# Retention and gated convolution on one core: a SyncE wait between a visit's y groups, whole columns in unit 0, and a new order from a corrected planner

## The chip, the cores and the metric

One core of one Trainium2 chip. The metric is the device time of one execution in microseconds; of several runs the median counts.

## The reference

Two stages, cut to what matters. First a retention layer with 4 batches, 8 heads, 768 tokens and 64 dimensions; then a gated MLP on its output, with 512 channels:

```python
for t in range(S):
    state = gamma * state + einsum('bhd,bhe->bhde', k[:, :, t], v[:, :, t])
    y[:, :, t] = scale * einsum('bhd,bhde->bhe', q[:, :, t], state)
x = y.transpose(0, 2, 1, 3).reshape(B, S, H * D)
gate = sigmoid(causal_conv(x, conv_w))        # five taps, each channel alone
out = (gate * (x @ w_val)) @ w_out
```

All inputs and the output are float32.

## The kernel before

The 768 tokens are cut into six chunks of 128, and with four batches that makes 24 pairs of batch and chunk, g = 0 to 23, taken chunk by chunk. All four batches of one chunk are a unit of 512 tokens for the MLP, so there are six units.

*Retention.* A pair of chunk 0 (g = 0 to 3) has a short form: `first_scores` (32 small products), a mask on VectorE, `first_y` (32 products), an evacuation into x on VectorE (`evac`), and `first_state`. Every later pair is a **visit**: `visit` does the 32 products of the masked scores with v, y's first group (`y_scores`, line 480 in the trace), then 16 products that complete this pair's state and 16 for the next pair's (line 464); then `rest_of_visit` adds y's second group, 32 products of the state with q (`y_state`, line 480 as well, since both call `y_mm`), and the next pair's 32 scores (line 407). In chunk 5 a visit has only the next pair's 16 state products, and the last visit has none. Both groups add into the same PSUM columns, from different rows of the array, so the second may begin only when the first is complete. The step `turn` sees to that: ScalarE copies two columns of y into a small tile that nobody reads, and TensorE waits for it.

*The MLP.* x is split into a high and a low part of TensorE's fast float32 format: ScalarE casts (`round_x`), GpSimd subtracts (`rest_x`). Four val tiles for each unit (`val_tile`) have 12 matmuls of 512 columns each: high by high, low weight by high, high weight by low. Unit 0 is in HALVED: its tiles are made as 24 matmuls of 256 columns (`val_half`, line 706), the first 12 of which need batches 0 and 1 alone. The convolution has one tap on ScalarE and four on VectorE (line 679), then comes a sigmoid on ScalarE, and VectorE multiplies it into the val tile's bank (line 715). The gated tile is split again. Units 0 and 5 have four output tiles (line 820); units 1 to 4 have seven products of half size (line 777), which need sums of blocks of w_out (`t_sums_at`) and buffers named top, from which the result is also sent. Two PSUM banks named mm serve val tiles, products and output tiles in turn.

*Loads.* SyncE issues all loads but two small ones. `LOADS` is the list of the first ones: ("q", g) is a pair's q and transposed k (0.5 MB), ("v", g) and ("k", g) 0.25 MB each, ("w", n) a weight block (0.5 MB; 0 to 3 are w_val's, 4 to 7 w_out's), "t" the table of masks and decays. A visit's step is followed by the two loads of the pair four ahead, and before the first of them stands a tiny DMA named passed (line 374), which makes SyncE wait until the visit has been evacuated.

*The order* of every engine is written out when the kernel is built. `WORK` is a string with one letter for each block of work: s, y, z for the first scores, y and state, p for the position product, w a weight load, h the head of the first visit, v a visit, V a val tile, T the sums of w_out, O an output tile or product. It gives each step a due time; `plan` then lists all steps as a simulation with the constants at the top of the file places them, and puts fillers (products into unused columns) into TensorE's gaps in the first stage. `fetch` and `run_pe` are its model of TensorE's instruction supply.

Of the kernel before, what the change touches and what calls it, by code (L numbers as in the profile page):

```python
# [7 lines left out]
F32 = mybir.dt.float32  # L8
# [8 lines left out]
P = 128  # L17
# [16 lines left out]
LO, HI = slice(0, HALF), slice(HALF, P)  # L34
# [1 line left out]

PAIR = 0.0145
MM = 0.2325
INTO, OUT_OF = 0.3, 0.134
COLD, WARM_AT = 1.85, 5.0  # L40
FIRST_PAGE, PAGE = 71, 127.6
FETCH, AHEAD, BEHIND, WORST = 3.3, 0.5, 1.5, 6.5
FIRST_BYTE, PER_MB = 2.95, 2.52
LATE_MB, LATE = 0.75, 1.85
TABLES = (4.6, 4.6)
SENT, SLACK = (2.8, 0.4), 1.5
HALVED = (0,)

TIMES = {
    "DVE": (0.69, 0.60),  # L50
# [8 lines left out]
FILLED_VALS = 48  # L59
CONV_LEAD, CHUNK = 7.0, 3.4  # L60
LOADS = (
    ("q", 0), ("t", 0), ("q", 1), ("v", 0), ("q", 2), ("w", 3), ("w", 0), ("v", 1),
    ("v", 2), ("v", 3), ("q", 3), ("k", 0), ("w", 1), ("w", 2), ("k", 2), ("k", 1),
    ("k", 3),
)

WORK = (
    "sspysyysyzzwzVwwhvVVzVwvOOOTvOvVvvVVvvVOVVvV"
    "VOvOOvvOOOOVVVvOOvOOOOvVvVOVvOOOVVvOOvOOOvVO"
    "OOVOVVOOOOO"  # L70
)

SEEN = {"DVE": 0.035, "ACT": 0.035, "POOL": 0.08, "PE": 0.08}
# [31 lines left out]
def plan(steps, filler, last, into):  # L105
# [46 lines left out]
    left = [0] * len(steps)  # L152
# [8 lines left out]
    while ends:  # L161
        t = ends.pop()
# [17 lines left out]
        if not s.waits:  # L180
            offer(s)
    order, landed, moved = [], 0.0, 0.0
    left, crossed, kind, sent = float(FIRST_PAGE), -9.0, "big", []

    def fetch(now):

        nonlocal left, crossed
        queued = max((x for t, x in sent if t <= crossed + AHEAD), default=0.0)
        crossed = now = max(now, min(max(crossed + FETCH, queued + BEHIND), crossed + WORST))
        left += PAGE  # L190
        return now

    def run_pe(s, now):
        nonlocal left, kind
        slow = COLD if now < WARM_AT else 1.0
        if s.small:
            if kind == "big":
                now += INTO
            kind = "small"
            todo, each = s.small, PAIR * s.wide * slow  # L200
        else:
            if kind == "small":
                now += OUT_OF
            kind = "big"
            todo, each = s.big, s.gap / max(1, s.big) * slow
        while todo > left:
            now += left * each
            todo -= left
            left = 0.0
            now = fetch(now)  # L210
        left -= todo
        now += todo * each
        return now, now + (0.21 if s.small else 0.17) * slow

# [2 lines left out]
    def quiet(ring):  # L217

        ends = [[s.end for s in users[k]] for k, w in rings.get(ring, ()) if w.end is not None]
        return max((1e9 if e is None else e for x in ends for e in x), default=0.0)  # L220

    def offered(e):
        return free[e] if e != "PE" or held is None else [s for s in free[e] if s is held]
# [18 lines left out]
    while any(free.values()):  # L242
        start, _, e = min(
            (round(max(clock[e], min(max(s.ready, s.own if s.engine == e else 0.0) for s in offered(e))), 6), e, e)
            for e in free
            if offered(e)
        )
        s = min(
            (s for s in offered(e) if max(s.ready, s.own if s.engine == e else 0.0) <= start + 1e-6),
            key=lambda s: (round(s.rank, 6), s.index),  # L250
        )
        if e == "PE":
            held = s.hold
            shut = shut or s.shut
            filling = filling and s is not last and s.hold is None
            ring = min(into[shut:], key=quiet)
            since = max(clock["PE"], quiet(ring))
            for i in range(int((start - since) * FILLED / FILL) if filling else 0):
                f = Step(0, "PE", FILL, [], [], filler, (ring,))
                f.start = since + i * FILL  # L260
                f.end = f.free = f.start + FILL
                order.append(f)
                left = max(0.0, left - (2 if ring == into[0] else 4))
        free[s.engine].remove(s)
        if s.other:
            free[s.other[0]].remove(s)
            if s.engine != e:
                s.engine, (s.cost, s.gap), s.fn = s.other
        s.start = start
        order.append(s)  # L270
        if e == "PE":
            clock[e], end = run_pe(s, start)
        elif e == "DMA":
            clock[e] = start + 0.45
            if moved <= LATE_MB < moved + s.mb:
                landed += LATE
            moved += s.mb
            landed = end = max(landed, start + FIRST_BYTE) + s.mb * PER_MB
            sent.append((start, landed))
            end += SLACK * (start > 30.0)  # L280
        else:
            if s.two:
                start = s.start = max(start, clock["POOL"])
                clock["POOL"] = max(clock["POOL"], start + s.gap)
            clock[e], end = start + s.gap, start + s.cost
            if s.mb:
                landed = max(landed, start + FIRST_BYTE - 0.6) + s.mb * PER_MB
                sent.append((start, landed))
        done(s, end)
        if s.turn:  # L290

            t, e = s.turn, s.turn.engine
            free[e].remove(t)
            t.start = max(clock[e], start + 0.49 + 32 * PAIR)
            clock[e] = t.start + t.gap
            order.append(t)
            done(t, t.start + t.cost)
# [5 lines left out]
def tile_retention_gated_mlp(  # L303
# [9 lines left out]
    nc = tc.nc  # L313
# [7 lines left out]
    const = ctx.enter_context(tc.tile_pool(name="const", bufs=1))  # L321
# [7 lines left out]
    ps_a = ctx.enter_context(tc.tile_pool(name="ps_a", bufs=2, space=PSUM))  # L329
    ps_m = ctx.enter_context(tc.tile_pool(name="ps_m", bufs=2, space=PSUM))  # L330

    turned = const.tile([P, 2, 1], F32, name="turned")
    small_sb = const.tile([P, small.shape[1]], F32, name="small_sb")
    vd_sb = small_sb[:, 0:48].rearrange("p (c x) -> p c x", x=8)
    ra_sb = small_sb[:, 48:72].rearrange("p (c x) -> p c x", x=4)
# [13 lines left out]
    sy = ps_y.tile([P, 2, 512], F32, name="sy")  # L349
# [10 lines left out]
    def at(due, engine, cost, reads, writes, fn, *args):  # L360
        steps.append(Step(due, engine, cost, list(reads), list(writes), fn, args))
        return steps[-1]
# [164 lines left out]
    def turn(g):  # L527


        nc.scalar.copy(turned[HI], sy[HI, :, 256:257])  # L530

    def rest_of_visit(g):
        y_state(g)
# [385 lines left out]
    def attention(g, t):  # L919

        b, c = chunks[g]
        qk, vk = ("att", g % LB, "qk"), ("att", g % LB, "vk")
        u, y = us_of.pop(g), Slot("y", 1)
        n = 32
        if g + 1 < NG:
            decay_at(t - 0.01, g + 1)
            taken[g + 1] = [Slot("snap", 4), Slot("snap", 4)]
            at(t - 0.005, "ACT", TIMES["snap"], ["z"], taken[g + 1][0:1], snap, g + 1, 0)
            n += 16
        if c < NCH - 1:  # L930
            n += 16
        step = at(t, "PE", 1.0, [u, vk] + ([("att", (g + 1) % LB, "vk")] if g + 1 < NG else []), [y, "z"], visit, g)
        step.small = n
        step.turn = at(t + 0.5, "ACT", (0.25, 0.2), [y], ["turn"], turn, g)
        reads, writes = [qk, "turn"] + taken[g], [y]
        if g + 1 < NG:
            scored[g + 1] = Slot("sc", 1)
            reads.append(("att", (g + 1) % LB, "qk"))
            writes.append(scored[g + 1])
        step.hold = at(t + 1.0, "PE", 1.0, reads, writes, rest_of_visit, g)  # L940
        step.hold.small = 64 if g + 1 < NG else 32
        if g + 1 < NG:
            scored_at(t + 1.01, g + 1)
        if b == 0:
            xbufs[c] = Slot("x", XB)
            last = [xbufs[c - 1]] + [("x", c - 1, i) for i in range(B)]
            at(t + 0.5, "ACT", (0.25, 0.15), last, [xbufs[c]] + [("x", c, i) for i in range(B)], new_x, c)
        at(t + 1.9, "DVE", TIMES["DVE"], [y, ("dec", c % 2), xbufs[c]], [("x", c, b)], evac, g)
        if c + 1 < NCH:
            at(t + 2.4, "ACT", (0.4, 0.3), ["base", "small"], [("dec", (c + 1) % 2)], table, c + 1, b)  # L950
        split(c, b, t + 1.95)
        whole[c] = t + 2.0
# [73 lines left out]
    def val_tile(n, m, t):  # L1026
        bank = Slot("mm", 2)
        gate_of = gates[n, m]
        halved = n in HALVED
        for z in range(3 * NPAIR * (1 + halved)):  # L1030
# [127 lines left out]
    for p, (kind, n) in enumerate(LOADS):  # L1158
        t = 0.1 * p
        if kind == "t":  # L1160
            at(t, "DMA", 0.4, [], ["small"], get, small_sb, small, nc.sync).mb = 0.2
        elif kind in "qrvk":
            load_part_at(t, n, *{"q": (0, 2), "r": (2, 4), "v": (2, 3), "k": (3, 4)}[kind])
        else:
            load_w_at(t, n)
# [12 lines left out]
    t, whole = 6.0, {}  # L1178
    now = dict.fromkeys("psyzvVOT", 0)
    now["h"] = now["v"] = B  # L1180
    now["w"] = len(early)
    for what in WORK:
# [7 lines left out]
        elif what == "s":  # L1190
            t = max(t, 6.0 + CHUNK * i)
# [138 lines left out]
```

## Time and profile before

| | |
|---|---|
| median of 3 runs | 207.59 us (205.69 to 209.82) |
| profiled execution | 206.92 us |
| its span, first to last instruction | 205.1 us |
| TensorE busy | 196.1 us, 96% |
| VectorE, ScalarE, GpSimd busy | 64%, 55%, 68% |
| DMA | 36.28 MB, mean 177 GB/s |

The span is what the trace shows; 1.8 us of the execution lie around it. Matmuls overlap, and their ends are modelled, so how fast a group of them runs is read from the starts of its members, or from the chain of waits, where each piece ends at the next one's start.

### The profile page before, as it was taken

The numbers are of one execution on the slowest core, as the hardware profiler recorded it, in microseconds if no ns is written. First come the engines' busy times: TensorE is split into PE (matmuls) and PEld (weight loads), VectorE is DVE, ScalarE is ACT, GpSimd is POOL, SyncE is SP. The second block draws the span as 40 slices with busy tenths as digits, with TensorE's granted clock in tenths as the row PEclk, the third lists the DMA queues.
The fourth block names the chain that finished last, engine by engine and source line by source line (L and its number), as shares of the span: only waits on it lengthen the run. The fifth ranks groups of instructions, "written<-read, shape, count | busy, mean of one in ns | idle before, by whom it ended". The sixth has DMA issues, their size and how long they took to land.

```text
span 205.1 us, 8324 instructions
## 1 busy us (share of the span) xinstructions
PE 196.1 (96%) x3688; PEld 167.4 (82%) x3688; DVE 131.2 (64%) x200; ACT 113.6 (55%) x245; POOL 140.1 (68%) x120
## 2 busy tenths in 40 slices
PE   8888989999999999999999899999999999999994
PEld 2576878878888879888999689988888889888883
DVE  1375987930489968992559795559992448994100
ACT  4198699754697558862555824236682237612221
POOL 0049949999997784999999738248999199222500
PEclk9999999999999999999999999999999999999999
DMA  6999994385595756344069520779001013112022
GB/s 199 367 410 411 414 415 168 107 291 227 151 328 176 270 211 220 135 141 190 3 225 316 189 96 6 258 187 328 5 13 44 0 54 105 51 63 91 0 105 104
DMA packets 14648, 36.28 MB, mean 177 GB/s; under 512 B 1554, under 2 KB 6034, under 8 KB 14612
## 3 DMA queue, kind: packets, MB, share of 16 engines
q1 hardware_dynamic: 8816, 29.43, 40.1%
q10 hardware_dynamic: 5796, 6.32, 8.7%
q8 instruction: 29, 0.48, 0.9%
q14 instruction: 7, 0.06, 0.1%
HBM read 29.46 MB, written 6.29 MB: 174 GB/s over the span
## 4 chain that ended last, share of the span: by engine, by line
PE 74%; DMA 17%; DVE 4%; ACT 1%; issue 1%; SPq 1%; ACTq 0%; DVEq 0%
PE mm L694 28%; PE mm L777 18%; PE mm L820 11%; PE sy L480 11%; DMA qk<-in_att_dram 6%; DMA wst<-in_w_dram 5%; PE sy L407 4%; DMA vk<-in_att_dram 4%; PE z_ps L464 4%; DMA out_dram<-top 2%; DVE acc L679 2%; SPq L383 1%; DVE u L429 1%; DVE x L622 1%; DVE x L560 0%
## 5 line engine op out<-in xcount | busy, mean ns | idle before, releaser
L679 DVE SCALAR_TENSOR_TENSOR acc<-x,cw_sb,acc 128x512 f32<-128x512 f32 x96 | 67.8, 751 | 4.3 <-ACT acc L677 3.7
L575 POOL TENSOR_TENSOR xl<-x,xh 128x512 fp32r<-128x512 f32 x24 | 31.0, 1291 | 22.9 <-ACT xh L570 22.9
L762 POOL TENSOR_TENSOR gvl<-gate,gvh 128x512 fp32r<-128x512 f32 x24 | 30.8, 1293 | 9.2 <-ACT gvh L758 9.2
L396 POOL TENSOR_TENSOR vk<-vk,small_sb 128x512 f32<-128x512 f32 x24 | 25.1, 1047 | 1.9 <-PE z_ps L464 1.3
L694 PE MATMUL mm<-xl,wvh 128*128 128x512 f32 x80 | 25.8, 395 | 0.0
L560 DVE TENSOR_TENSOR x<-sy,dec 128x512 f32<-128x512 f32 x20 | 13.7, 687 | 18.7 <-PE sy L407 17.7
L694 PE MATMUL mm<-xh,wvh 128*128 128x512 f32 x80 | 25.5, 403 | 0.0
L715 DVE TENSOR_TENSOR gate<-mm,gate 128x512 f32<-128x512 f32 x24 | 16.4, 688 | 13.7 <-PE mm L694 11.3
L694 PE MATMUL mm<-xh,wvl 128*128 128x512 f32 x80 | 24.2, 399 | 0.0
L745 POOL TENSOR_TENSOR gate<-gate 128x512 f32<-128x512 f32 x16 | 20.6, 1292 | 3.9 <-DVE gate L715 3.7
L758 ACT CAST gvh<-gate 128x512 fp32r<-128x512 f32 x24 | 14.7, 625 | 13.2 <-DVE gate L715 10.0
L570 ACT CAST xh<-x 128x512 fp32r<-128x512 f32 x24 | 14.9, 621 | 8.2 <-DVE x L560 7.3
L687 ACT ACTIVATE gate<-acc 128x512 f32<-128x512 f32 x24 | 14.3, 599 | 8.7 <-DVE acc L679 4.5
L726 POOL TENSOR_TENSOR gvl<-gate,gvh 128x512 fp32r<-128x512 f32 x8 | 10.3, 1290 | 12.6 <-ACT gvh L722 12.6
L694 PEld LDWEIGHTS mm<-xh,wvl 128*128 128x128 f32 x80 | 14.8, 188 | 3.3
L694 PEld LDWEIGHTS mm<-xl,wvh 128*128 128x128 f32 x80 | 14.9, 188 | 3.0
L429 DVE TENSOR_TENSOR u<-sy,small_sb 128x512 f32<-128x512 f32 x20 | 13.7, 685 | 5.6 <-PE sy L407 5.6
L677 ACT ACTIVATE acc<-x,cw_sb 128x512 f32<-128x512 f32 x24 | 16.4, 691 | 1.4 <-DVE x L560 1.1
L694 PEld LDWEIGHTS mm<-xh,wvh 128*128 128x128 f32 x80 | 14.3, 188 | 3.2
L530 ACT COPY turned<-sy 64x2 f32<-64x2 f32 x20 | 3.1, 156 | 23.5 <-PE sy L480 17.7
L475 ACT COPY snap<-z_ps 128x256 f32<-128x256 f32 x40 | 14.2, 376 | 3.2 <-PE z_ps L464 1.6
L464 PE MATMUL z_ps<-vk 64*64 64x64 f32 x704 | 14.8, 219 | 0.4 <-issue 0.4
(83 smaller groups left out, 410.6 us busy)
## 6 DMA issues: line engine op xcount, KB each, us to landing
qk<-in_att_dram SPq DMA_DIRECT2D x24, 512.0 KB, 5.7
vk<-in_att_dram SPq DMA_DIRECT2D x20, 512.0 KB, 5.0
wst<-in_w_dram SPq DMA_DIRECT2D x8, 512.0 KB, 8.4
out_dram<-o_sb ACTq DMA_DIRECT2D x15, 256.0 KB, 2.7
vk<-in_att_dram SPq DMA_DIRECT2D x8, 256.0 KB
out_dram<-top ACTq DMA_DIRECT2D x8, 256.0 KB, 4.2
passed<-x SPq DMA_DIRECT2D x16, 0.0 KB
out_dram<-gate ACTq DMA_DIRECT2D x2, 128.0 KB, 1.7
```

What stands on the lines that cost most here:

```text
L396: nc.gpsimd.tensor_tensor(v, v, vd_sb[:, c, :].unsqueeze(2).broadcast_to([P, 8, HALF]), op=ALU.mult)
L464: nc.tensor.matmul(z_ps[cols, x, b, j], lhsT=k[rows, x, j, s, :], rhs=v[rows, x, j, s, :], start=g == 0 and s == 0 and j == 0, stop=True, ...
L480: nc.tensor.matmul(sy[cols, h, off:off + HALF], lhsT=lhsT, rhs=rhs, start=start, stop=True, skip_group_check=True,)
L575: nc.gpsimd.tensor_tensor(xl[n][:, :, b], xs[n][:, :, b, HALO:], xh[n][:, :, b].bitcast(F32), op=ALU.subtract)
L677: nc.scalar.mul(acc, x[:, :, 0:P], cw_sb[:, m, 0:1])
L679: nc.vector.scalar_tensor_tensor(acc, x[:, :, k:k + P], cw_sb[:, m, k:k + 1], acc, op0=ALU.mult, op1=ALU.add,)
L694: nc.tensor.matmul(vps[n, m], lhsT=w[:, m, ct * P:(ct + 1) * P], rhs=xx[n][:, ct].rearrange("p b t -> p (b t)"), start=(i == 0), stop=(i = ...
L715: nc.vector.tensor_tensor(gv, vps.pop((n, m)), gv, op=ALU.mult)
L745: engine.tensor_tensor(block(n, k), block(n, a), block(n, b), op=getattr(ALU, op))
L762: engine.tensor_tensor(low, block(n, k), operands[n, k, 0].bitcast(F32), op=ALU.subtract)
L777: nc.tensor.matmul(banks[bank][:, tt * 256:(tt + 1) * 256], lhsT=g[:, ct, tt * P:(tt + 1) * P], rhs=weight(w, part % 2)[:, ct], start=(k i ...
L820: nc.tensor.matmul(ops[n, b, cs.start][:, 0:cs.stop - cs.start], lhsT=gg[:, b * P:(b + 1) * P], rhs=w[:, ct, cs], start=(i == 0), stop=(i ...
```

## The change

- `turn` no longer copies. An empty SyncE instruction reads the same two columns, as far as dependences go; TensorE's second group waits for SyncE's semaphore. The planner counts the step on the DMA queue, at 0.1 us in place of ScalarE's 0.25.
- HALVED is empty: unit 0's val tiles use 512 columns like the others.
- The planner's model of the instruction supply is another (fetches are asked for at a page's end and become usable later), its constants for loads and for the small table are changed.
- LOADS and WORK are other orders of the same steps.

```diff
-INTO, OUT_OF = 0.3, 0.134
+INTO, OUT_OF = 0.25, 0.134
-FETCH, AHEAD, BEHIND, WORST = 3.3, 0.5, 1.5, 6.5
-FIRST_BYTE, PER_MB = 2.95, 2.52
-LATE_MB, LATE = 0.75, 1.85
+LEAD, AHEAD, BEHIND, WORST, USABLE, DEPTH = 1.0, 0.0, -0.95, 4.5, 2.35, 23
+FIRST_BYTE, PER_MB = 2.85, 2.65
+LATE_MB, LATE = 1.0, 1.7
-SENT, SLACK = (2.8, 0.4), 1.5
-HALVED = (0,)
+SENT, SLACK = (3.4, 0.4), 0.7
+HALVED = ()
 LOADS = (
-    ("q", 0), ("t", 0), ("q", 1), ("v", 0), ("q", 2), ("w", 3), ("w", 0), ("v", 1),
-    ("v", 2), ("v", 3), ("q", 3), ("k", 0), ("w", 1), ("w", 2), ("k", 2), ("k", 1),
-    ("k", 3),
+    ("q", 0), ("t", 0), ("q", 1), ("w", 0), ("q", 2), ("v", 1), ("v", 0), ("v", 2),
+    ("v", 3), ("q", 3), ("w", 1), ("k", 1), ("k", 0), ("w", 2), ("k", 3), ("w", 3),
+    ("k", 2),
 )
 WORK = (
-    "sspysyysyzzwzVwwhvVVzVwvOOOTvOvVvvVVvvVOVVvV"
-    "VOvOOvvOOOOVVVvOOvOOOOvVvVOVvOOOVVvOOvOOOvVO"
-    "OOVOVVOOOOO"
+    "spssyysyyzwVzwVVwwzzhVvOOvvOvOVvTVvVvVvOVVOv"
+    "vVvOOOVvOVOVOvOOOVvOOOvvVOVVVOOOOOvOOOOvOvO"
+    "vVOVOVVOOOO"
 )
...
     def fetch(now):
-        nonlocal left, crossed
-        queued = max((x for t, x in sent if t <= crossed + AHEAD), default=0.0)
-        crossed = now = max(now, min(max(crossed + FETCH, queued + BEHIND), crossed + WORST))
-        left += PAGE
+        nonlocal left, need, usable, later
+        if left <= 1e-9:
+            asked = max(now, usable)
+            queued = max((x for t, x in sent if t <= asked + AHEAD), default=0.0)
+            later = min(max(asked + LEAD, queued + BEHIND), asked + WORST) + USABLE
+            left = PAGE
+        else:
+            now = max(now, usable)
+            usable, need = later, PAGE
         return now
...
     def turn(g):
-        nc.scalar.copy(turned[HI], sy[HI, :, 256:257])
+        nc.sync.keepalive_nop([nc.sync.lower_ap(sy[HI, :, 256:257])])
...
-        step.turn = at(t + 0.5, "ACT", (0.25, 0.2), [y], ["turn"], turn, g)
+        step.turn = at(t + 0.5, "DMA", (0.1, 0.0), [y], ["turn"], turn, g)
...
-            at(t, "DMA", 0.4, [], ["small"], get, small_sb, small, nc.sync).mb = 0.2
+            at(t, "DMA", 0.4, [], ["small"], get, small_sb, small, nc.sync).mb = 0.07
```

Written out by blocks (V1.2 is unit 1's third val tile, O2.0 unit 2's first product, v8 the visit of g = 8), the new order begins s p s s y y s y y z w V0.0 z w V0.1 V0.2 w w z z h V0.3 v4 O0.0 O0.1 v5 v6 O0.2 v7 O0.3 V1.0, where the old one has s s p y s y y s y z z w z V0.0 w w h v4 V0.1 V0.2 z V0.3 w v5 O0.0 O0.1 O0.2 T v6 O0.3 v7 V1.0. Around the end of unit 1 the old one has O1.4 O1.5 O1.6 O2.0 V3.0, the new one O1.5 V3.0 O1.6 V3.1 O2.0. Neighbouring visits are v5 v6, v12 v13 and v18 v19 in the new order; O3.6 O4.0 are neighbours in both.

## Rows read from the trace of the kernel before

**Rows 1.** The page: busy us by engine, and the chain that ended last.
```profile
PE 196.1 (96%) x3688; PEld 167.4 (82%) x3688; DVE 131.2 (64%) x200; ACT 113.6 (55%) x245; POOL 140.1 (68%) x120
...
PE 74%; DMA 17%; DVE 4%; ACT 1%; issue 1%; SPq 1%; ACTq 0%; DVEq 0%
```

**Rows 2.** Busy time by stage: stretch, length, engines' busy us, clock, DMA share, GB/s.
```profile
5.00:20.00 15.00, 12.65 (x283) 9.60 (x283) 7.85 (x13) 9.80 (x22) 6.41 (x6) 1.00 1.02 394
20.00:42.10 22.10, 20.87 (x530) 19.12 (x530) 18.98 (x29) 18.48 (x38) 19.02 (x17) 1.00 0.71 275
42.10:202.10 160.00, 158.34 (x2878) 137.31 (x2870) 103.50 (x158) 82.77 (x180) 114.44 (x95) 1.00 0.42 144
```

**Rows 3.** The start in order of time: start us, us, engine, line, tiles, [idle <-releaser].
```profile
10.85 0.90 PE L497 MATMUL z_ps<-u,vk 64*64 64x128 f32 x32
...
15.94 1.23 PE L420 MATMUL sy<-qk 64*64 64x128 f32 x32 [0.30 <-DMA qk<-in_att_dram]
...
17.10 0.74 PE L706 MATMUL mm<-xh,wvh 128*128 128x256 f32 x4
...
19.18 0.69 DVE L560 TENSOR_TENSOR x<-z_ps,base 128x512 f32<-128x512 f32 x1 [1.02 <-PE z_ps L497]
...
20.60 0.74 PE L706 MATMUL mm<-xh,wvl 128*128 128x256 f32 x4
...
22.78 0.61 ACT L570 CAST xh<-x 128x512 fp32r<-128x512 f32 x1
...
28.68 0.74 PE L706 MATMUL mm<-xh,wvh 128*128 128x256 f32 x4 [0.89 <-DVE gate L715]
```

**Rows 4.** Two stretches of val matmuls in order of time: weight loads, matmuls.
```profile
24.25 1.00 PEld L706 LDWEIGHTS mm<-xh,wvl 128*128 128x128 f32 x8
25.18 1.00 PEld L706 LDWEIGHTS mm<-xl,wvh 128*128 128x128 f32 x8
...
179.44 1.09 PE L694 MATMUL mm<-xh,wvh 128*128 128x512 f32 x4
180.38 0.87 PE L694 MATMUL mm<-xh,wvl 128*128 128x512 f32 x3
```

**Rows 5.** The tile turned: ns min/median/max, first and last start.
```profile
L530 ACT COPY turned<-sy x20: 155/155/157, 36.3 to 168.3; 64x2 f32<-64x2 f32 x20
```

**Rows 6.** The chain that ended last in order of time: start, us, what.
```profile
41.17 0.55 PE sy L480 x32
...
50.21 0.50 PE sy L480 x31
...
144.79 0.69 PE sy L480 x32
```

**Rows 7.** Two visits in order of time, at 72 us and the last one.
```profile
71.70 0.68 DVE L560 TENSOR_TENSOR x<-sy,dec 128x512 f32<-128x512 f32 x1
...
72.41 0.60 SPq L374 DMA_DIRECT2D passed<-x  x1
...
72.64 0.69 PE L480 MATMUL sy<-u,vk 64*64 64x64 f32 x32
...
73.51 0.42 SPq L383 DMA_DIRECT2D vk<-in_att_dram  x1
73.66 0.57 PE L480 MATMUL sy<-qk,snap 64*64 64x64 f32 x22
...
74.53 0.29 PE L480 MATMUL sy<-qk,snap 64*64 64x64 f32 x4 [0.29 <-issue]
...
168.52 0.69 PE L480 MATMUL sy<-qk,snap 64*64 64x64 f32 x32 [0.32 <-ACT turned L530]
```

**Rows 8.** Unit 2's first product in order of time.
```profile
113.36 0.59 ACT L786 COPY top<-mm 128x512 f32<-128x512 f32 x1 [1.24 <-DMA out_dram<-top]
...
114.00 0.74 PE L777 MATMUL mm<-woh,gvh 128*128 128x256 f32 x4 [0.90 <-ACT top L786]
```

More of the change, by code (lines that the diff above doesn't have):

```diff
@@ L61 @@
 LOADS = (
-    ("q", 0), ("t", 0), ("q", 1), ("v", 0), ("q", 2), ("w", 3), ("w", 0), ("v", 1),
-    ("v", 2), ("v", 3), ("q", 3), ("k", 0), ("w", 1), ("w", 2), ("k", 2), ("k", 1),
-    ("k", 3),
+    ("q", 0), ("t", 0), ("q", 1), ("w", 0), ("q", 2), ("v", 1), ("v", 0), ("v", 2),
+    ("v", 3), ("q", 3), ("w", 1), ("k", 1), ("k", 0), ("w", 2), ("k", 3), ("w", 3),
+    ("k", 2),
 )
 WORK = (
-    "sspysyysyzzwzVwwhvVVzVwvOOOTvOvVvvVVvvVOVVvV"
-    "VOvOOvvOOOOVVVvOOvOOOOvVvVOVvOOOVVvOOvOOOvVO"
-    "OOVOVVOOOOO"
+    "spssyysyyzwVzwVVwwzzhVvOOvvOvOVvTVvVvVvOVVOv"
+    "vVvOOOVvOVOVOvOOOVvOOOvvVVOVVVOOOOOvOOOOvOvO"
+    "vVOVOVVOOOO"
 )
@@ L182, in plan @@
     order, landed, moved = [], 0.0, 0.0
-    left, crossed, kind, sent = float(FIRST_PAGE), -9.0, "big", []
+    left, need, usable, later = float(FIRST_PAGE), float(FIRST_PAGE + DEPTH), 0.0, 0.0
+    kind, sent = "big", []
     def fetch(now):
-        nonlocal left, crossed
-        queued = max((x for t, x in sent if t <= crossed + AHEAD), default=0.0)
-        crossed = now = max(now, min(max(crossed + FETCH, queued + BEHIND), crossed + WORST))
-        left += PAGE
+        nonlocal left, need, usable, later
[7 more added lines that the diff above has]
+            usable, need = later, PAGE
         return now
     def run_pe(s, now):
-        nonlocal left, kind
+        nonlocal left, need, kind
         slow = COLD if now < WARM_AT else 1.0
@@ L205, in run_pe @@
             todo, each = s.big, s.gap / max(1, s.big) * slow
[L206 to L209, printed above, removed]
+        while todo > min(left, need):
+            x = min(left, need)
+            now += x * each
+            todo -= x
+            left -= x
+            need -= x
             now = fetch(now)
         left -= todo
+        need -= todo
         now += todo * each
@@ L262, in plan @@
                 order.append(f)
-                left = max(0.0, left - (2 if ring == into[0] else 4))
+                x = min(left, 2.0 if ring == into[0] else 4.0)
+                left -= x
+                need -= x
         free[s.engine].remove(s)
@@ L330, in tile_retention_gated_mlp @@
     ps_m = ctx.enter_context(tc.tile_pool(name="ps_m", bufs=2, space=PSUM))
-    turned = const.tile([P, 2, 1], F32, name="turned")
     small_sb = const.tile([P, small.shape[1]], F32, name="small_sb")
```

## Prediction

> **What bounds the kernel now.** I read the page's busy times and chain first, then the busy time by stage, then the start in order of time, and last the few places where TensorE waits later on. TensorE is busy for 196.1 us of a 205.1 us span, and the chain that ended last is mostly TensorE, with a DMA share of 17% [rows 1]. By stage [rows 2] the kernel falls in two. From 42.1 to 202.1 us TensorE is busy for 158.34 of 160 us: not 2 us are idle, so there a new order of the same work can win back little more than that and the waits inside the visits. The start is another kernel: from 5 to 20 us the DMA engines are full (394 GB/s) and TensorE's time goes to small first products and fillers; from 20 us on it is busy for 20.87 of 22.10 us. The granted clock is 1.00 in every stage. So I look for the change in three places: the start, the few waits after it, and the new instruction inside the visits.
>
> **The start, loads first.** Unit 0's first stage ends with chunk 3. Its scores start at 15.94 us, released by the landing of its qk load; its evacuation on VectorE runs from 19.18 to 19.87 [rows 3]. The loads are one stream, so a load's place is the bytes ahead of it. In the old list, up to and with ("q", 3), lie four q (2.0 MB), four v (1.0), two w (1.0) and the small table (0.07): 4.07 MB. In the new list there is one w less: 3.57 MB. At 394 GB/s [rows 2] the 0.5 MB are 1.27 us, by which the end of the first stage comes earlier: **-1.3 us**. Two things limit that. ("v", 0) moves from fourth to seventh place, 1.25 MB or 3.2 us later, under the first y product, which ran only at 10.85 us [rows 3] because the position product stood ahead of it; the new order has that product in second place, so I let the two cancel. And the bytes of all loads before the first visits are the same, so what depends on the last weight isn't earlier.
>
> **Whole columns in place of halves.** Eight half matmuls take 0.93 us (24.25 to 25.18, start to start), so two halves cost 0.233 us; four whole ones take 0.94 us (179.44 to 180.38), 0.235 each [rows 4]. The columns themselves win and lose nothing. What is lost is the early start: a half needs two chunks, a whole column four. In the old run 4 halves ran at 17.10 and 8 more at 20.60, before ScalarE had cast chunk 3; that cast came at 22.78, 2.9 us after the evacuation [rows 3]. If ScalarE casts at once, only the first four are lost, 4 x 0.116 = 0.5 us; if it is as late as before, all twelve, 1.4 us. I take **+0.5 us**, near the prompt cast, because the new order has one weight less to convert at that point.
>
> **The hold at 28.68 us.** There TensorE waits 0.89 us until VectorE has multiplied the first gate [rows 3]: both banks are full, and the multiplication waits for the convolution, which needs all four chunks. The new order has two val tiles back to back there as well, but the convolution comes 1.3 us earlier with the chunks, while the first tile starts later. I let half of it go: **-0.4 us**; bounds 0 and -0.89. The start together: **-1.2**; bounds +1.4 (the late cast, and nothing gained) and -2.5 (the loads, and all of the 1.2 us that TensorE is idle from 20 to 42.1).
>
> **The wait inside a visit.** Now y's first group ends, ScalarE copies two columns, and TensorE may go on. The copy takes 155 ns each time [rows 5]. With 32 state products between the groups it is nearly hidden: in the chain of waits a second group takes 0.50 us where nothing is late (50.21), and 0.55 in seven of the sixteen such visits (41.17). In chunk 5, with 16 state products, it takes 0.69 in all three visits [rows 6], and in the last visit, with none, 0.69 after 0.32 us idle [rows 7]. So 7 x 0.05, 3 x 0.19 and 0.51 are what the wait costs, 1.4 us. The new wait has no copy; what an empty SyncE instruction costs is in no row. From below: SyncE starts a DMA issue at 72.41, 0.03 us after the VectorE write that releases it (71.70 + 0.68) [rows 7], so it reacts at once, and the most that can go is the copy: 0.155 in four visits and 0.05 in seven, -1.0. From above: SyncE's queue is in order, and it holds three DMA issues for the chunk four ahead, 72.41 to 73.93, 1.5 us. What releases them is the evacuation of the visit before, which the next visit needs as well, so they never hold the new wait for long; but they occupy SyncE. At 72.64 a visit began beside them; its second group started at 73.66, while SyncE was still issuing until 73.93 [rows 7]. There the new wait would cost 0.3 us more than the copy did. I take **-0.6**; bounds -1.0 and +0.9 (0.3 in each of the three pairs of neighbouring visits of the new order, nothing gained). ScalarE also loses the idle time ahead of the copies; it is busy for 55% of the span [rows 1], and I count nothing for that.
>
> **The stall at 113 us.** In the old order unit 2's first product follows unit 1's last directly. Its copy out of the bank needs the buffer from which unit 1's block is being sent: ScalarE waits 1.24 us for that send, copies from 113.36, and TensorE goes on at 114.00 after 0.90 us idle [rows 8]. In the new order a val tile (12 x 0.235 = 2.8 us) stands between the two, and another ahead of the last product. **-0.9**; bounds 0 (it comes back between units 3 and 4, whose last and first products stay neighbours) and -0.9.
>
> **Instruction supply and new stalls.** At 74.53 the second group of a visit stops in its middle for 0.29 us, and the trace finds no semaphore that it waited for [rows 7]. I read it as a late fetch of instructions, which is what the planner's new model is about; that model acts only by order and fillers. A new order has its own such places. I add one more of these and a margin for a wait that I don't foresee, **+0.4**; bounds -0.3 (this one gone, no other) and +1.0 (three).
>
> The Trainium skill, "Runtime: NRT & Kernel Launch", section "Instruction fetch mechanics", says that crossing into the next block of instructions is "mostly hidden", since dispatch is slower than the refill. The gap speaks against that here; by the page the term would be near 0.1 and the time 0.3 us less.
>
> **Sum.** -1.2 - 0.6 - 0.9 + 0.4 = -2.3 us. The profiled execution took 206.92 us (205.1 of span and 1.8 around it); the median of the three runs is 207.59. From the first that is 204.6, from the second 205.3. I forecast **204.8 us**.
>
> **Rivals.** First, *the start closes up*: the cast comes at once, the hold goes, TensorE is full from the first val product on. For it: all of its inputs but the weights come 1.3 us earlier, and 1.2 us are idle from 20 us on. Against it: GpSimd, which makes the low parts that the products need, is busy for 19.02 of the same 22.10 us [rows 2]. It gives 206.92 - 2.5 - 1.0 - 0.9 - 0.3 = 202.2. Second, *nothing arrives*: TensorE starts earlier and waits for GpSimd or for the last weights, and the late cast takes what the loads gave. Then the stall's 0.9 and little else remain, against +1.4 and new stalls: 206 to 208.4, say 207. For it: the same 19.02 us, and the cast at 22.78 [rows 3], which was late for no lack of data. Third, on the other side, *SyncE's issues stand ahead of the wait*: where a visit's first group ends within the 1.5 us that three issues take, TensorE waits for the last of them, 0.3 us as at 73.66. If the planner puts the issues ahead in all 16 visits that have them, that is 16 x 0.32 = 5.1 us: 206.92 + 5.1 = 212.0; it decides, against the gains of the others, from about ten visits on. For it: one visit in the old order stood just so [rows 7]. Against it: the issues follow their visit at once, and most visits have products for several microseconds between them.
>
> **How the numbers follow.** Forecast 0.50, closed start 0.20, nothing 0.25, SyncE 0.05. The range reaches over the first three with some of the runs' own spread (205.69 to 209.82): 201.6 to 208.5. About 2%, 4.2 us, is what a measurement of this kernel can tell from no change: faster by more is under 203.4, slower by more over 211.7. Faster: most of the closed start and a tenth of the forecast, 0.24. Slower: 0.06. Between: 0.70.
>
> **What would show it.** In the new profile: chunk 3's scores near 14.7 us; the first val product soon after 19 us; no copy between a visit's groups, and chunk 5's second groups near 0.55 us in place of 0.69; where DMA issues stand beside a visit, a gap of 0.3 or none; no product that waits for a sent block. From 42 us on TensorE should be as full as it is. I am wrong if the start doesn't move because ScalarE or GpSimd is late with chunk 3's parts, or if the second groups wait behind SyncE's DMA issues.

## The result and the profile after

The changed kernel takes 204.94 us (median of 20 runs, 202.65 to 207.78), the kernel before 207.35 us in runs beside it; the ratio is 0.987 [0.9838, 0.9901], some 2.7 us (ratios here leave out the slower state into which some runs of either kernel fall). A second set of six runs, e10 below, gave 0.9891 [0.9844, 0.9938]. The time is the one forecast, 204.8; its parts are not. The profiled execution took 204.64 us.

Page of the changed kernel, busy us by engine and the chain that ended last, beside [rows 1]:

```profile
PE 196.4 (97%) x3648; PEld 165.6 (82%) x3648; DVE 131.4 (65%) x200; ACT 109.3 (54%) x225; POOL 140.3 (69%) x120
...
PE 94%; DMA 3%; DVE 1%; issue 0%; SPq 0%; ACT 0%; ACTq 0%
```

ScalarE has lost 20 instructions, the copies, and TensorE 40 (48 val matmuls fewer, a few fillers more). The chain is TensorE's own to 94%, where the DMA engines had 17%. By stage, in the columns of [rows 2], with one stretch more:

```profile
8.00:11.00 3.00, 3.00 (x36) 2.61 (x36) 1.56 (x2) 2.12 (x6) 0.00 (x0) 0.50 1.04 405
...
20.00:42.10 22.10, 21.88 (x453) 17.17 (x455) 19.44 (x30) 19.29 (x38) 20.20 (x18) 1.00 0.72 275
```

From 20 us on TensorE is as good as full: the hold of 0.89 us [rows 3] is gone. Yet the first stage ended no earlier in this execution. The start in order of time, beside [rows 3], and below it one DMA issue of SyncE's that the visits come to:

```profile
7.88 1.51 PE L432 MATMUL sy<-qk 64*64 64x128 f32 x32 [1.05 <-DMA qk<-in_att_dram]
...
13.28 0.90 PE L509 MATMUL z_ps<-u,vk 64*64 64x128 f32 x32
...
15.00 0.90 PE L509 MATMUL z_ps<-u,vk 64*64 64x128 f32 x32 [0.81 <-DVE x L572]
...
15.86 0.90 PE L432 MATMUL sy<-qk 64*64 64x128 f32 x32
...
19.57 0.69 DVE L572 TENSOR_TENSOR x<-z_ps,base 128x512 f32<-128x512 f32 x1 [0.42 <-PE z_ps L509]
20.85 0.60 ACT L582 CAST xh<-x 128x512 fp32r<-128x512 f32 x1
21.90 0.94 PE L706 MATMUL mm<-xh,wvh 128*128 128x512 f32 x3
...
78.69 1.28 SPq L395 DMA_DIRECT2D vk<-in_att_dram  x1
```

The second chunk's load came late, TensorE waited 1.05 us for it and then ran the same 32 products in 1.51 us at half the clock: 0.50 was granted from 8 to 11 us, the first of the two stretches above. The first y product stands at 13.28 us, where it stood at 10.85. Chunk 3's evacuation begins at 19.57 in place of 19.18. That this start is not the kernel's usual one is shown below. The visits, from the chain that ended last, beside [rows 6]: an ordinary one, one that stands beside a DMA issue of SyncE's, one of chunk 5, and the last:

```profile
46.89 0.62 PE sy L492 x32
47.52 0.47 PE z_ps L476 x32
47.98 0.47 PE sy L492 x32
...
79.54 0.51 PE z_ps L476 x30
...
80.07 0.03 SPq L542
...
80.14 0.69 PE sy L492 x32
...
142.36 0.62 PE sy L492 x32
142.98 0.23 PE z_ps L476 x16
143.22 0.59 PE sy L492 x32
...
168.47 0.67 PE sy L492 x32
...
169.22 0.69 PE sy L492 x32
```

A second group takes 0.47 us, where it took 0.50 or 0.55, and 0.59 in chunk 5, where it took 0.69. In the last visit the wait costs 0.08 us in the chain (168.47 + 0.67 is 169.14, then 169.22), where the chain of before has 0.27 (168.25 to 168.52); the 0.32 of [rows 7] is the same wait read as TensorE's idle time. No product waits for a sent block any more: TensorE's waits for top, 0.90 us in [rows 8], have no entry among its waits of over 0.2 us.

### The profile page after: what moved, and what is told of

It is laid out like the page before. It is cut to its first block, busy times and chain, and to the rows that moved or that the text cites. A ratio compares the mean times of both kernels' runs of the same rounds, so it can differ in the third digit from the quotient of the medians.

```text
span 202.9 us, 8260 instructions
## 1 busy us (share of the span) xinstructions
PE 196.4 (97%) x3648; PEld 165.6 (82%) x3648; DVE 131.4 (65%) x200; ACT 109.3 (54%) x225; POOL 140.3 (69%) x120
## 4 chain that ended last, share of the span: by engine, by line
PE 94%; DMA 3%; DVE 1%; issue 0%; SPq 0%; ACT 0%; ACTq 0%
PE mm L706 34%; PE mm L789 21%; PE mm L832 12%; PE sy L492 11%; PE z_ps L476 6%; PE sy L419 5%; DMA qk<-in_att_dram 3%; PE z_ps L509 2%; PE sy L432 2%; PE z_ps L864 2%; PE sy L864 1%; DVE x L572 1%; SPq L398 0%; SPq L395 0%; ACT gate L845 0%
## 5 line engine op out<-in xcount | busy, mean ns | idle before, releaser
L706 PE MATMUL mm<-xh,wvh 128*128 128x512 f32 x96 | 31.5, 404 | 0.0
L706 PE MATMUL mm<-xl,wvh 128*128 128x512 f32 x96 | 31.3, 399 | 0.0
L706 PE MATMUL mm<-xh,wvl 128*128 128x512 f32 x96 | 26.8, 395 | 0.0
L706 PEld LDWEIGHTS mm<-xh,wvl 128*128 128x128 f32 x96 | 17.9, 188 | 3.9
L582 ACT CAST xh<-x 128x512 fp32r<-128x512 f32 x24 | 14.9, 622 | 11.3 <-DVE x L572 11.3
L706 PEld LDWEIGHTS mm<-xl,wvh 128*128 128x128 f32 x96 | 17.7, 188 | 3.7
L706 PEld LDWEIGHTS mm<-xh,wvh 128*128 128x128 f32 x96 | 17.3, 188 | 3.6 <-ACT o_sb L813 0.2
L789 PE MATMUL mm<-wst,gvh 128*128 128x256 f32 x96 | 15.7, 286 | 0.0
```

Source lines behind the costliest of these rows:

```text
L706: nc.tensor.matmul(vps[n, m], lhsT=w[:, m, ct * P:(ct + 1) * P], rhs=xx[n][:, ct].rearrange("p b t -> p (b t)"), start=(i == 0), stop=(i = ...
L789: nc.tensor.matmul(banks[bank][:, tt * 256:(tt + 1) * 256], lhsT=g[:, ct, tt * P:(tt + 1) * P], rhs=weight(w, part % 2)[:, ct], start=(k i ...
```

## Experiments

Two sums come up in several places. *A visit's length* is the time from its first y product to the start of the last product of y's second group, from the trace. *Counted work* adds up TensorE's products in their order, each at the pace of its kind in an undisturbed stretch (0.2325 us for 512 columns, 0.1185 for 256, 0.0145 and 0.0218 for the small ones), without fillers; I read when 26 and 170 us of it are done. Unit 0 in halves counts 0.2 us more than in whole columns, so starts of the two kinds compare only to within that. The first point lies at about 43 us, when the start is over, the second near the end.

### The wait alone, and the copy back

In the kernel before, nothing but the copy is changed (e2); in the changed kernel, nothing but the empty instruction (e1):

```diff
-        nc.scalar.copy(turned[HI], sy[HI, :, 256:257])
+        nc.sync.keepalive_nop([nc.sync.lower_ap(sy[HI, :, 256:257])])
```

> The kernel before with the empty SyncE instruction in place of the copy, nothing else changed. Theory: visits of 1.41 us, 1.30 in chunk 5, except where SyncE is still issuing loads (the visit that started at 72.64 us, one or two more, 0.2 to 0.3 us longer); the time 0.8 to 1.4 us under before, ratio 0.993 to 0.996. Rival (SyncE's issues stand ahead of the wait often enough to eat it): several visits of 1.7 us and a ratio of 0.998 to 1.003.

> The changed kernel with ScalarE's copy back in place of the empty SyncE instruction; all other instructions stay in the changed kernel's order. Theory (the copy's 155 ns and what hangs on it were on TensorE's path in nearly every visit): from the first y product to the last of the second group a visit takes 1.45 to 1.49 us again in place of 1.41, in chunk 5 1.45 in place of 1.30, and the time is 1.2 to 1.5 us over the changed kernel, ratio to before 0.993 to 0.995. Rival (the visits got shorter because of the order around them): visits stay at 1.41 and the time stays within 0.4 us of 204.9, ratio 0.987 to 0.989.

e2 took 205.22 us, ratio 0.9905 [0.987, 0.994]: 2.0 us from this line alone, more than its theory's 0.8 to 1.4. e1 took 206.36 us, ratio 0.9972 [0.9935, 1.001], so the copy costs the changed kernel 1.4 us of median, and its visits are longer again as the theory said. The chains of e2 and then of e1 at a visit of chunk 5:

```profile
142.14 0.62 PE sy L480 x32
142.76 0.23 PE z_ps L464 x16
143.00 0.59 PE sy L480 x32
```

```profile
143.35 0.67 PE sy L492 x32
144.02 0.02 issue
144.04 0.02 ACTq L542
144.06 0.04 issue
144.10 0.16 ACT turned L542
144.26 0.04 issue
144.30 0.69 PE sy L492 x32
```

With the copy the chain goes through ScalarE, 0.28 us from 144.02 to 144.30, and the 16 state products hide only part of that; without it TensorE runs through. An undisturbed visit's length is 1.45 to 1.50 us with the copy and 1.41, in chunk 5 and in the last visit 1.30, without. Of before, less the fetch gap, the 20 visits sum to 29.35 us; 16 x 1.41 + 4 x 1.30 = 27.76, so **1.6 us** are to be had where nothing disturbs the new wait. In e2's profile two visits did meet SyncE's issues: at 39.22 and 62.13 us the second group starts 1.15 and 1.27 us after the first product, in place of 0.98. The visit at 72 us, which the prediction feared, starts it at 0.98.

### What an empty instruction costs, and an issue ahead of it

Nine empty instructions in place of one (e6), and an empty one, a tiny DMA and another empty one (e7):

```diff
-        nc.sync.keepalive_nop(...)
+        [nc.sync.keepalive_nop(...) for _ in range(9)]                                   # e6
+        nc.sync.keepalive_nop(...); nc.sync.dma_start(out=held_row, in_=small_sb[0:1, 0:1]); nc.sync.keepalive_nop(...)  # e7
```

> The changed kernel with nine empty SyncE instructions in place of one in each visit; the order of everything else is the same. It prices one of them. If one costs some 0.05 us, eight more make 0.4 us: chunk 5's second groups start 1.2 us after the first in place of 0.83, ordinary ones 1.2 in place of 0.98, and the time is 4 to 6 us longer (ratio 1.005 to 1.015). If one costs 0.02 us or less: chunk 5's at most 1.0, ordinary ones unchanged or 0.1 later, the time at most 1 us longer (ratio 0.987 to 0.992). Its start is also a second look at the changed kernel's: with the loads at their usual pace the first y product comes at 11.6 us, as in the run with the copy back, and not at 13.28.

> The changed kernel with one tiny DMA issued on SyncE in each visit between two empty instructions, both of which wait for y's first group, so that the wait is held by exactly one DMA issue. The prediction's third rival said that an issue in SyncE's queue holds TensorE for as long as it takes. By it every visit is 0.35 to 0.6 us longer from the first group to the second (0.83 to 1.2 or 1.4 in chunk 5, 0.98 to 1.2 or 1.4 elsewhere), and the time is 6 to 10 us over the changed kernel, 211 to 215. If SyncE can pass on while an issue is under way: under 0.1 us a visit, 205 to 207.

e6 took 213.53 us, ratio 1.0343 [1.0277, 1.0409]. Over the changed kernel that is 8.6 us for 160 instructions, 0.054 us each, and more than the 4 to 6 us expected; in chunk 5 second groups begin 0.53 us later, 0.066 for each of the eight, in most other visits 0.40 us later, 0.050 each. One empty instruction is thus well under the 0.155 us of the copy [rows 5]. e7 took 216.21 us in a single run. A visit of it in order of time:

```profile
46.92 0.69 PE L492 MATMUL sy<-u,vk 64*64 64x64 f32 x32
47.44 0.65 PE L476 MATMUL z_ps<-vk 64*64 64x64 f32 x32
47.81 0.59 SPq L542 DMA_DIRECT2D held_row<-small_sb  x1
...
48.51 0.69 PE L492 MATMUL sy<-qk,snap 64*64 64x64 f32 x32 [0.43 <-SPq L542]
```

SyncE issues from 47.81 to 48.40, and only then does its queue come to the instruction on which TensorE waits: the second group begins 0.6 us late, 20 times over, 11.3 us in all. The third rival's mechanism is real and its price of 0.3 us was low; what spares the changed kernel is the place of the issues. One visit of 20 met one, at 79 us: the issue that stands last in the start's fence above runs from 78.69 to 79.97, and TensorE goes on at 80.14, 1.30 us after its first product in place of 0.98. It is 0.32 us, the rival's figure. In the second profile of the same kernel (e10, below) that issue took 0.44 us in place of 1.28, and the visit lost nothing.

### A val tile between unit 1's last product and unit 2's first

In the string of the kernel before one O and one V change places (e5):

```diff
-    "VOvOOvvOOOOVVVvOOvOOOOvVvVOVvOOOVVvOOvOOOvVO"
+    "VOvOOvvOOOVOVVvOOvOOOOvVvVOVvOOOVVvOOvOOOvVO"
```

> The kernel before with one letter pair of the order exchanged, so that a val tile stands between unit 1's last and unit 2's first product. Theory (the 0.9 us wait there is for the sent block's buffer, and the changed kernel lost it by its order alone): no wait for a copy of top near 113 us, the work after it 0.9 to 1.1 us earlier against the same kernel's earlier places, the time 0.5 to 1.1 us under before, ratio 0.9945 to 0.9975. Rival (another buffer is late next, since the send takes as long): a wait of over 0.4 us within the next ten us, ratio 0.998 to 1.002.

205.44 us, ratio 0.9915 [0.9876, 0.9953]. TensorE's waits have no entry for top, and six microseconds of counted work around that place (86 to 92) took 6.45 us where the kernel before took 7.43: **1.0 us**, and nothing came back between units 3 and 4. From 26 to 170 us of counted work e5 takes 154.00 us, before 155.35; the 0.35 us beyond the 1.0 are spread over other places. The ratio is beyond the theory's range, but e5's profile is also 0.65 us ahead at 26 us, before the exchanged place, so a part of the difference is not of this change.

### The changed kernel once more, and its loads

The changed kernel itself (e10), then with ("v", 0) in its old fourth place (e3, and e9 once more), then with the old list of loads (e4):

```diff
-    ("q", 0), ("t", 0), ("q", 1), ("w", 0), ("q", 2), ("v", 1), ("v", 0), ("v", 2),
+    ("q", 0), ("t", 0), ("q", 1), ("v", 0), ("q", 2), ("v", 1), ("w", 0), ("v", 2),
```

> The changed kernel itself, once more, for the run beside it and for a second profile of its start. Theory A (the pace of the first loads in the first profile of it was an exception): the first y product near 11.4 us in place of 13.28, chunk 3's evacuation at 18.3 to 18.6, the granted clock 1.00 from 5 to 15 us, second groups as before at 0.98 us after the first product of a visit. Rival B (the order itself makes the loads late): first y again at 13 us or later and the clock under 0.9 there. Time 204.9 us in both, ratio to before 0.987.

> The changed kernel with (v, 0) and (w, 0) exchanged in the list of loads, so that v of chunk 0 is fourth again. Theory (the new order lost at the start because the first y product waited for v of chunk 0 until 13.3 us, and the four y products follow each other at 1.7 us): first y product at 10 to 11 us in place of 13.28, chunk 3's evacuation 1 to 1.7 us earlier than 19.57, and the time 0.7 to 1.5 us under the changed kernel, ratio 0.980 to 0.984. Rival (the start is set by the weights and GpSimd, not by the first y): the first y comes earlier and the first visit does not; ratio 0.986 to 0.988.

> The changed kernel with ("v", 0) in its old fourth place and ("w", 0) in the seventh, a second time with more rounds. Theory A (the late v0 costs what it delays): y's products follow each other from the first on, so with v0 earlier the first stage ends earlier; this kernel stands 0.3 to 0.6% under the changed kernel run beside it, near 203.7 us. Rival B (eaten): an instruction gap and the cast set the end of the stage in both orders, the two agree within 0.3%, near 204.9 us. In both the first y product runs near 10.1 us, and chunk 3's evacuation ends B at 18.1 to 18.6, A under 18.

> The changed kernel with the list of loads of the kernel before. The prediction's step (a load of weights less ahead of chunk 3 brings the end of the first stage 1.3 us forward): without it chunk 3's scores come later, and the time is about 1.2 us over the changed kernel, ratio 0.992 to 0.994. The theory of the late first y: the new list gained nothing, so the time is equal or up to 0.8 us less, ratio 0.983 to 0.988.

e10: 204.01 us, ratio 0.9891 [0.9844, 0.9938]. Its start in order of time:

```profile
7.45 0.90 PE L432 MATMUL sy<-qk 64*64 64x128 f32 x32 [0.37 <-DMA qk<-in_att_dram]
...
11.49 0.90 PE L509 MATMUL z_ps<-u,vk 64*64 64x128 f32 x32
...
13.20 0.90 PE L509 MATMUL z_ps<-u,vk 64*64 64x128 f32 x32 [0.81 <-DVE x L572]
...
14.07 0.90 PE L432 MATMUL sy<-qk 64*64 64x128 f32 x32
...
16.28 0.68 PE L509 MATMUL z_ps<-u,vk 64*64 64x128 f32 x23 [0.83 <-issue]
...
18.73 0.69 DVE L572 TENSOR_TENSOR x<-z_ps,base 128x512 f32<-128x512 f32 x1 [0.42 <-PE z_ps L509]
...
20.01 0.60 ACT L582 CAST xh<-x 128x512 fp32r<-128x512 f32 x1
...
21.06 1.18 PE L706 MATMUL mm<-xh,wvh 128*128 128x512 f32 x4
```

So the late start of the first profile is not the order's; e1, e6 and e7, with the same start, have the first y product at 11.2 to 11.6 us too. Of the 1.8 us between the two profiles (13.28 against 11.49), 0.43 came with the load (7.88 against 7.45) and 1.37 with the clock: the same 32 products and the six fillers behind them took 3.95 us (to 11.83) in place of 2.58 (to 10.03). Here chunk 3's scores run at 14.07, 1.9 us earlier than in [rows 3], more than the 1.3 forecast. But its evacuation begins only 0.45 us earlier: y's products follow each other at 1.7 us, since each waits for VectorE to clear the bank of the one before, the chain begins later by the late v0, and a gap in the instruction supply breaks the third (what ties such gaps to the supply stands in the account below). From the second y product to the evacuation the first profile, which has no gap there, takes 4.57 us (15.00 to 19.57), e10 5.53 (13.20 to 18.73). So by these rows the gap costs about 1.0 us, an estimate, and without it the stage would have ended 1.4 us earlier than before.

With v0 earlier, e3 took 203.51 us, ratio 0.9815 [0.9753, 0.9877], from six runs, inside its theory's range; e9, the same kernel with twelve, 204.16 us, 0.9875 [0.9835, 0.9915], beside 204.01 for e10. By that it is not shown to be better than the changed kernel. The start of e9:

```profile
10.39 0.85 PE L509 MATMUL z_ps<-u,vk 64*64 64x128 f32 x32
...
12.12 0.90 PE L509 MATMUL z_ps<-u,vk 64*64 64x128 f32 x32 [0.88 <-DVE x L572]
...
15.88 0.88 PE L509 MATMUL z_ps<-u,vk 64*64 64x128 f32 x27 [0.70 <-issue]
...
18.52 0.69 DVE L572 TENSOR_TENSOR x<-z_ps,base 128x512 f32<-128x512 f32 x1 [0.42 <-PE z_ps L509]
```

The first y product is 1.1 us earlier, fillers take the room, the gap comes in the third y product again, and chunk 3's evacuation is 0.2 us earlier: rival B held. e4, with the old list under the new order, took 204.98 us, ratio 0.9931 [0.9894, 0.9967]; chunk 3's scores stand at 16.62 us after 1.40 us of waiting for their load, and 26 us of counted work are done at 44.47, 1.4 us after e10. The ratio is where the prediction's step put it: under the new order the new list helps the start. Over the whole run that is 0.4 to 0.6% by the ratios, with intervals that overlap, and 0 to 1.0 us by the medians (204.94 and 204.01 for the changed kernel).

### Halves and whole columns

The changed kernel with halves (e8), and the kernel before with whole columns (e11):

```diff
-HALVED = ()        # e8
+HALVED = (0,)
-HALVED = (0,)      # e11
+HALVED = ()
```

> The changed kernel with unit 0's val tiles in halves again (planned anew with that alone). The prediction's term says whole columns lose 0.5 us, up to 1.4: with halves the first val product comes about 3 us earlier, the first visit 0.5 to 1.4 us earlier, ratio 0.980 to 0.985. Rival (nothing lost: the stage's end is set by the weights, GpSimd and VectorE): the first visit within 0.3 us of the changed kernel's, ratio 0.985 to 0.990.

> The kernel before with unit 0's val tiles in 512 columns, all else as it was. Theory A (my term): the early half matmuls at 17.10 and 20.60 have nothing in their place, the first val product begins only after chunk 3's cast, and the time is 0.5 us longer (up to 1.4), ratio 1.002 to 1.007. Rival B (whole columns cost nothing, since VectorE's first gate and GpSimd's low parts set the start of the next tiles): the later first tile shortens the hold at 28.7 us by as much as it comes later, ratio 0.998 to 1.001.

e8 took 206.43 us, ratio 0.9992 [0.9946, 1.0038], 1.2% over the changed kernel: the opposite of my term. Its profile has the same late start as the first of the changed kernel (first y product at 13.28 and a clock of 0.50 from 8 to 11 us in both), so the two starts compare: 14 us of counted work are done at 29.04 against 30.39, the twelve early halves' 1.4 us; 20 us at 36.40 against 37.36; 26 us at 43.73 against 43.93. The halves start early, and then wait for banks: TensorE's waits of e8 have 0.8 us for the gate and 0.6 for GpSimd's scaled k, which the changed kernel has not. So whole columns cost next to nothing by the end of the start. The rest of e8's loss is elsewhere, 1.3 us of it one gap in the instruction supply near 101 us.

e11 took 214.34 us, ratio 1.0378 [1.0324, 1.0431]; neither theory had that. The start costs 1.7 us (26 us of counted work at 45.10 against 43.38), more than the worst I had allowed. The rest are stalls that the kernel before does not have, or has shorter (0.9 us for top, 0.3 for the copy), from TensorE's waits (us in total, times, longest):

```profile
PE sy L480 <- ACT turned L530: 2.0, 3, 1.5
PE mm L694 <- issue: 1.4, 1, 1.4
PE mm L777 <- ACT top L786: 1.2, 1, 1.2
PE mm L777 <- issue: 0.9, 1, 0.9
```

The longest wait for the copy, by ScalarE's instructions and the product behind them in order of time:

```profile
112.07 0.69 PE L480 MATMUL sy<-u,vk 64*64 64x64 f32 x32
112.17 0.62 ACT L570 CAST xh<-x 128x512 fp32r<-128x512 f32 x1
...
112.69 1.30 ACT L677 ACTIVATE acc<-x,cw_sb 128x512 f32<-128x512 f32 x2
...
113.92 0.23 ACT L554 COPY x<-x 128x64 f32<-128x64 f32 x1
114.06 0.40 ACT L547 ACTIVATE dec<-base,small_sb 128x128 f32<-128x128 f32 x1
114.48 0.16 ACT L530 COPY turned<-sy 64x2 f32<-64x2 f32 x1
114.69 0.52 PE L480 MATMUL sy<-qk,snap 64*64 64x64 f32 x20 [1.46 <-ACT turned L530]
```

Y's first group is ready at about 112.7; the copy stands behind five other steps in ScalarE's queue and runs at 114.48. A copy on a busy engine costs its place in the queue, here nine times its own duration; the string of the kernel before had kept that place good, and the plan built from the same string with another HALVED did not.

### The planner alone

The kernel before with the new constants and `fetch`, the old lists, halves and copy (e12).

> The kernel before, built with the changed planner: new constants and the new model of the instruction supply, but the old loads, the old string of work, the halves and ScalarE's copy. Theory A (my assumption that the model acts only by order and fillers): the same time within 0.5%, the visits at 0.97 to 1.02 us to the second group, a gap in the instruction supply of 0.3 to 1.5 us somewhere as in the other runs. Rival B (the corrected model places fillers so that such gaps go): no gap over 0.2 us from 20 us on, and 0.5 to 1 us less.

210.02 us, ratio 1.0179 [1.0119, 1.0238]: neither. The start is no worse (20 us of counted work at 36.11, before 36.60), but from 26 to 170 us it takes 158.12 us against 155.35: gaps of 0.70 and 0.44 in the supply, waits for top of 1.5 us in three places where before had 0.9 in one. Less the gap of 0.29 us and the wait that before has, that is about half of the 2.8 us; the rest is not traced. My assumption that the model acts only by order and fillers stands; what the order makes of it was wrong by 1.8%.

## Why the time was right and the parts were not

Counted work, us at which so much is done. Before, e2 and e5 share one start, the changed kernel, e10, e6 and e1 another (up to 20 us, before the visits' wait differs):

| | 20 us | 26 us | 170 us | 26 to 170 |
|---|---|---|---|---|
| before | 36.60 | 43.38 | 198.73 | 155.35 |
| e2, wait alone | 35.77 | 42.74 | 196.70 | 153.96 |
| e5, val tile between | 36.09 | 42.73 | 196.73 | 154.00 |
| changed, first profile | 37.36 | 43.93 | 196.66 | 152.73 |
| e10, changed again | 36.51 | 43.09 | 195.35 | 152.26 |
| e9, v0 fourth | 36.30 | 42.99 | 194.82 | 151.83 |

- **The start, -1.2: failed; it gives nothing.** The old start has 20 us done at 35.77, 36.09 and 36.60, the new one at 36.07 (e1), 36.34 (e6), 36.51, and 37.36 in the profile with the late start. Chunk 3's load did come earlier, its scores by 1.9 us. The step that failed first is "by which the end of the first stage comes earlier": the chain of y's, with a gap in its third product, ended the stage, not chunk 3's load, and the evacuation begins only 0.45 us earlier (18.3 to 18.7 in four profiles, 19.0 to 19.5 in three with the old start). In e10 the gap alone costs about 1.0 us; the prediction had such gaps in a term apart, not on this path. "So I let the two cancel" failed too: they didn't, v0's place put the first y product half a microsecond later (11.2 to 11.6 us against 10.6 to 11.3). But with v0 back in its place, and the gap still there, the evacuation comes no more than a few tenths earlier (18.52 in e9, 18.13 in e3), so that is not the main loss. The step "I take +0.5 us, near the prompt cast" failed as well: the cast came 0.6 us after the evacuation, not at once, the first val product at 21.06 and not soon after 19, and all twelve early halves, 1.4 us, were lost at first. Most of them came back where the old start holds before the gate, 0.89, 0.39 and 0.28 us in its three profiles, and where e8 waits for banks. That hold going, -0.4, was right in sign and is part of the same account.
- **The wait in a visit, -0.6: right in mechanism, mis-sized.** It is -1.4 to -2.0 by the medians and ratios of e1 and e2, -1.6 by undisturbed visits; the bound of -1.0 was passed. The step that failed is "the most that can go is the copy: 0.155 in four visits and 0.05 in seven, -1.0". Its baseline, 0.50 us for a second group "where nothing is late", held a part of the copy's wait already: without the copy a group takes 0.47. So the visits that were counted at nothing got 0.04 shorter, the seven 0.08; the four got 0.14 to 0.19, as assumed. And -0.6 was set above -1.0 to allow for SyncE's issues, of which the changed kernel met one in its first profile and none in e10's.
- **The stall at 113 us, -0.9: right.** e5 has 1.0 us for it alone, and it did not come back between units 3 and 4.
- **Instruction supply, +0.4: unsettled in size.** That a gap without a semaphore is a late fetch was a reading. The trace's DMA records support it: TensorE's gaps of this kind can be set beside the blocks of 16 KB on the queue q8, of kind instruction, 28 or 29 in an execution. In the 14 profiles 24 gaps of over 0.15 us end 1.2 to 1.6 us after such a block has landed. In e10 blocks landed at 14.93 and 50.52 us and gaps end at 16.28 and 51.84; before, a block landed at 73.30 and the gap of [rows 7] ends at 74.53. Eleven profiles have one more, of 0.22 us near 20 us, at least 4.6 us after a block, which is something else. Without it the changed kernel has 0.2 us of such gaps in its first profile and 1.1 in e10's, of which 0.8 lie in the start; before 0.5. The Trainium skill, "Runtime: NRT & Kernel Launch", section "Instruction fetch mechanics", has a crossing "mostly hidden". By count the traces agree with that: of e10's 28 blocks two are followed by a gap, of e11's 28 five, of e2's 29 none. So the prediction's "The gap speaks against that here" claims too much; what one crossing costs when it is not hidden goes up to 1.42 us here (e11).
- **Sum.** After the start the changed kernel saves 2.6 and 3.1 us in its two profiles (152.73 and 152.26 against 155.35); e2 saves 1.39 there and e5 1.35, together 2.7. So wait and stall are about the whole gain, as far as two single changes can be added; no run has both in the old order. That the forecast met the time was luck: two errors, +1.2 and -1.0, nearly cancelled in it.
- **Rivals.** "The start closes up" half came: TensorE is full from 20 to 42.1 us (22.10 of 22.10 us in e10), but by starting val later. "Nothing arrives" described the start. "SyncE's issues" is shown by e7; it struck once in the first profile, not in e10's, and twice in e2.

No version beat the changed kernel beyond its interval. Two things stay open: the time that e11 and e12 lose cannot be put down to a single line of the planner, and why the first loads come late in some executions was not tried.

## What to carry to other kernels

Before pricing a wait that is removed, look whether the undisturbed case that serves as the baseline has that wait in it too: here every visit did, and the term came out at less than half. A load that lands earlier is worth only what the chain behind it can take: find the last link (here y after y through one bank, and a gap in the instruction supply within it) before counting the bytes. One part of a planned order, carried alone into the other order, is not measured by its time (whole columns +3.8%, planner +1.8%, while the whole change gains 1.3%); compare stretches of the traces instead.

## What the runs showed of the hardware

- An empty SyncE instruction between two groups of TensorE work costs 0.050 to 0.066 us in a row of nine; as a single wait it takes 0.08 us from the end of one group to the next in the last visit, where the ScalarE copy took 0.27 (before), and 0.28 in a visit of chunk 5 (144.02 to 144.30, e1).
- The same load list does not land at the same pace in every execution: the first y product stands at 11.2 to 11.6 us in four profiles and at 13.28 in two (the changed kernel's first, and e8). In those two TensorE stood idle for 1.05 and 1.13 us, waiting for the second chunk's load until 7.9 us, and the granted clock was 0.50, 1.2 GHz, from 8 to 11 us; the 32 score products behind the wait took 1.51 us where e10, waiting 0.37 us and at 1.00, 2.4 GHz, took 0.90. An idle stretch of that length did not always lower it: e4 waited 1.40 us for a load at about 16 us and kept 1.00.
- Gaps in which TensorE waits for no semaphore were 0.2 to 1.42 us long and stood elsewhere in most kernels. Of the 35 over 0.15 us in the 14 profiles, 24 end 1.2 to 1.6 us after a 16 KB block of instructions has landed; the other 11 are the one of 0.22 us near 20 us. The five behind such blocks in e11 (0.60 at 16.6 us, 0.22, 0.56, 1.42 and 0.93 later) add up to 3.7 us.
